# A hand-written order of issue for the first three units and the token weights, replaced by another

## The chip, the cores and the metric

The kernel runs on one core of one Trainium2 chip. The metric is device time in microseconds (us) for one launch; lower is better. Engines in the text: TensorE (PE; its weight loads are PEld), VectorE (DVE), ScalarE (ACT), GpSimd (POOL) and SyncE (SP), which issues almost all DMAs.

## What is computed

A linear attention with a decaying state (RWKV-6) feeds a mixer of two MLPs. Cut to what matters:

```python
batch, n_heads, seq, head_dim = (4, 8, 768, 48)
d_tok, d_ch = (256, 1536)
for t in range(S):
    kt, vt, rt, wt = (k[:, :, t], v[:, :, t], r[:, :, t], w[:, :, t])
    cur = np.einsum('bhd,bhe->bhde', u[None] * kt, vt)
    y[:, :, t] = np.einsum('bhd,bhde->bhe', rt, state + cur)
    state = wt[:, :, :, None] * state + np.einsum('bhd,bhe->bhde', kt, vt)
x = np.ascontiguousarray(attn_out.transpose(0, 2, 1, 3)).reshape(B, S, H * D)
xt = x.transpose(0, 2, 1)
h = np.maximum(xt @ w_tok1, 0.0) @ w_tok2
u = x + h.transpose(0, 2, 1)
h2 = np.maximum(u @ w_ch1, 0.0) @ w_ch2
return (u + h2).astype(np.float32)
```

Everything is float32, except that the four weights arrive as 64-bit floats and are put together on the chip from their bits.

## The kernel before

**Units.** The 768 tokens of a batch are cut into three units of 256; a unit holds 16 groups of 64 tokens for pairs of heads. `unit(i)` returns a unit's steps as small functions. On VectorE: `ends` (L372, a running product of the decays from the back, and a reciprocal), `keys` (L382), `begins` (L385, the running product from the front), `queries` (L388), `own_put` (L400), `mask` (L274), and `updates`, called s0, s1, s2 in the order, one for each of the four 64-token steps of the state (L445 to L453; the last unit has three). On ScalarE: `own_u` (L278, four multiplies), `copied` (L293, two copies of the turned keys), `scaled` (L438 to L443, called t0, t1, t2: four small multiplies each, between one update and the next), `seen` (L331), `taken` (L349, three copies of the result into x) and `ranges` (L366 to L369, two checks of the running product, whose sums are read at the very end). On TensorE: `own_gram` and `gram` (L262), `tokens` (L292, eight transposes), `carry` (L308, the outer products), `before` (L322, the products with the state) and `after` (L343, the products within the group). One update needs `carry` and the multiplies before it, and the next multiplies need the update, so a unit's state is a chain VectorE, ScalarE, VectorE, and so on.

**Banks.** During the first three units, PSUM has two double banks for gram and y (pool `ps_g`), two banks for the turned keys and the first product of the mixer (`ps_m`), and one for `carry` (`ps_a`). So `before` of unit 0 takes the bank that `mask` of unit 0 frees, `before` of unit 1 the one that `taken` of unit 0 frees, and `carry` of a unit waits for the last update of the unit before.

**Weights.** `convert` (L200) handles 512 KB times two of raw weights at a time. Its steps are load (two DMAs on SP), exponent x (DVE, L214), mantissa m (DVE, L220), power p (ACT, L217), sum add (DVE, L226), signs g (ACT, L223) and put (DVE, L229 and twice L232). `to_tok` has three of them, for the two token weights; `to_ch` has those for the channel weights, of which the first is in the hand-written order up to its signs. In the names x0, m0, p0, add0, g0, put0 the digit is the conversion; 3 is the first of `to_ch`. A load waits until the raw place that it fills has been read.

**Mixer of batch 0.** `hidden(i, c)` (L744) adds the product of 128 tokens (chunk c of six; a unit gives two) to one of two halves i, and is followed by a rectifier on ScalarE. In the list h the calls are h[2c + i]. `back(c)` (L751 to L756) needs both rectified halves, `turn` (L762, L763) transposes the result, `up` (L772) and `down` (L783) are the channel MLP.

**Order.** `strict` (L78) fixes the order of issue on TensorE, VectorE, ScalarE and SP to the order of the list it is given; each engine runs its own instructions in that order and waits where an operand is late. The call at L943 gives the order for units 0 to 2, the token weights and the first products of the mixer. After it, PSUM is divided anew into six banks, and `interleaved` (L854) merges three lists for batch 0: the mixer, the attention of batch 1 (units 3 to 5), and the channel weights, by a small model of engine times (costs in us, needs and banks written with each piece). In that merged part the next `ends` takes the place of a running product that the `ranges` of unit 1 read, which is why the planner was given `("of", 0)`.

Of the kernel before, what the change touches and what calls it, by code (L numbers as in the profile page):

```python
# [18 lines left out]
AF = mybir.ActivationFunctionType  # L19
# [4 lines left out]
C = S // 128  # L24
UC = 2
UB = C // UC
# [10 lines left out]
DTOK, DCH = 256, 1536  # L37
# [15 lines left out]
def rwkv6_then_mixer(  # L53
# [429 lines left out]
    rooms, forms, formed = {}, {}, {}  # L483
# [255 lines left out]
    def mixing(bt, x_of, out_rows):  # L739
        h1 = mpool.tile([128, DTOK // 128, DM], f32, name="h1", bufs=1)  # L740
        xT = mpool.tile([128, DM // 128, S], f32, name="xT", tag="xT", bufs=1)
        zs, sums = {}, {}

        def hidden(i, c):  # L744
            if c == 0:
                sums[i] = ps_m.tile([128, DM], f32, name="h1_ps", tag="m")
            pe.matmul(sums[i], now["wtok1"][:, c, ts(i, 128)], x_of()[:, c, :], start=(c == 0), stop=(c == C - 1))  # L747
            if c == C - 1:
                act.activation(h1[:, i, :], sums.pop(i), AF.Relu)

        def back(c):  # L751
            ps = ps_m.tile([128, DM], f32, name="h_ps", tag="m")
            for i in range(DTOK // 128):
                pe.matmul(ps, now["wtok2"][:, i, ts(c, 128)], h1[:, i, :], start=(i == 0), stop=(i == DTOK // 128 - 1))
            x = x_of()
            dve.tensor_add(x[:, c, :], x[:, c, :], ps)  # L756

        def turn(c):

            ps = bank("xT_ps")[:, :DM].rearrange("p (m t) -> p m t", t=128)  # L760
            for m in range(DM // 128):
                pe.transpose(ps[:, m, :], x_of()[:, c, ts(m, 128)], ident)  # L762
            act.copy(xT[:, :, ts(c, 128)], ps)  # L763

        def up(s, jt, blocks=range(DM // 128)):
            if jt == 0 and 0 in blocks:
                zs[s] = now["z"][int((bt, s) != (0, 0))].rearrange("p (j t) -> p j t", j=NJ)
            if 0 in blocks:
                sums["z", s] = ps_m.tile([128, SEG], f32, name="z_ps", tag="m")
            ps = sums["z", s]  # L770
            for m in blocks:
                pe.matmul(ps, now["wch1"][:, m, ts(jt, 128)], xT[:, m, ts(s, SEG)],  # L772
                          start=(m == 0), stop=(m == DM // 128 - 1))
            if DM // 128 - 1 in blocks:
                act.activation(zs[s][:, jt, :], ps, AF.Relu)

        def down(s, n, jts):

            if jts[0] == 0:
                sums[n] = ps_m.tile([128, DM], f32, name="h2_ps", tag="m")  # L780
            ps = sums[n]
            for jt in jts:
                pe.matmul(ps, zs[s][:, jt, ts(n, 128)], now["wch2"][:, jt, :], start=(jt == 0), stop=(jt == NJ - 1))  # L783
            if jts[-1] == NJ - 1:
                o = mpool.tile([128, 2, DM], f32, name="o", bufs=1) if n == 0 else sums["o"]
                sums["o"] = o
                dve.tensor_add(o[:, n], x_of()[:, 2 * s + n, :], ps)
                sp.dma_start(out_rows(2 * s + n), o[:, n])

        return dict(hidden=hidden, back=back, turn=turn, up=up, down=down)  # L790

    now["z"] = halves

# [3 lines left out]
    def attention_pieces(i):  # L797
# [6 lines left out]
        def piece(f, name, *ops):  # L804
            return (i, name), f, ops
# [5 lines left out]
            return pieces if i == UB else ()  # L811

        loads = piece(lambda: load_rk(i + 1), "loads")
        ends = piece(e["ends"], "ends", ("DVE", 2.6, last("small", "large", "by3") + ((("of", 0),) if i == UB else ())))
        keys = piece(e["keys"], "keys", ("DVE", 1.25, k("ends")))
        small, large = (piece(e["ranges"][n], name, ("ACT", 1.4, k("ends"))) for n, name in enumerate(("small", "large")))
        begins = piece(e["begins"], "begins", ("DVE", 2.35, k("ends")))
# [36 lines left out]
    def interleaved(mix, *others, room=0.6, hurry=0.04, lead=(0.01, 0.2)):  # L854
# [57 lines left out]
        while any(streams):  # L912
# [14 lines left out]

    turned = mixing_of(0)
    h = [lambda i=i, c=c: turned["hidden"](i, c) for c in range(C) for i in range(DTOK // 128)]
    to_tok = conversion((wtok1, w_tok1, 2, 256), (wtok2, w_tok2, 2, 256), rooms=lambda n: (n % 2, n % 2))  # L930
    to_ch = conversion((now["wch1"], w_ch1, 1, 512), (now["wch2"], w_ch2, 4, 128), rooms=lambda n: (n % 2, 0, rks[2][:, ts(n % 2, PIECE)].bitcast(bf16)) if n else (2, 1))
    to_tok[0][0]()
# [7 lines left out]
    in_turn.update({pe.engine: None, dve.engine: None, act.engine: None, sp.engine: None})  # L940
    s0, s1, s2 = (e["updates"] for e in (e0, e1, e2))
    t0, t1, t2 = (e["scaled"] for e in (e0, e1, e2))
    strict(*e0["own_u"], e0["ends"], e0["own_gram"], e0["begins"], e0["keys"], e0["tokens"], *e0["copied"], e0["queries"], lambda: load_w(2),  # L943
           e0["gram"], *e1["own_u"], e1["ends"], e0["carry"], *e0["ranges"], e0["own_put"], e0["mask"], e1["own_gram"], s0[0], t0[1],
           x0, p0, s0[1], t0[2], m0, g0, e1["begins"], s0[2], t0[3], add0, s0[3], t1[0], e0["before"], e0["seen"], put0, load2,
           e1["keys"], e0["after"], *e2["own_u"], e1["tokens"], *e1["copied"], e1["queries"], e1["own_put"], e1["carry"], *e0["taken"],
           lambda: load_v(2), e1["gram"], e2["ends"], g1, s1[0], t1[1], e2["keys"], e2["tokens"], s1[1], t1[2], e2["own_gram"], *e2["copied"],
           e2["begins"], s1[2], t1[3], e1["mask"], load3, s1[3], t2[0], *h[:2], e2["carry"], e1["before"], h[2], e2["queries"], s2[0], t2[1],
           e2["own_put"], e1["seen"], s2[1], t2[2], e2["gram"], x1, p1, e1["after"], m1, s2[2], t2[3], e2["mask"], h[3], add1,
           e1["taken"][0], put1, to_ch[1][0], lambda: (load_w(3), load_rk(3), load_v(UB)), e2["before"], e2["seen"], *e1["taken"][1:],  # L950
           x2, s2[3], e2["after"], *h[4:8], *e2["taken"], m2, p2, x3, add2, g2, m3, h[8], h[10], h[9], h[11], p3, put2, add3, g3,
           to_ch[2][0], e1["ranges"][0])

    six_banks.close()
    ps_g, ps_m = None, six_banks.enter_context(tc.tile_pool(name="ps_m", bufs=6, space=bass.MemoryType.PSUM))
# [56 lines left out]
    def weights_in_turn():  # L1012

        each = [single(steps, n) for n, steps in enumerate(to_ch)]
        for n in range(1, len(each) - 2):
            each[n].insert(-1, each[n + 2].pop(0))
        first = sum(each, [])
        stored = [(("kept", i), lambda i=i: sp.dma_start(kept[i], (wtok1, wtok2)[i].rearrange("p c k -> p (c k)")), ()) for i in range(2)]
        ranges = [(("of", n), f, (("ACT", 1.4, ()),)) for n, f in enumerate((e1["ranges"][1], *e2["ranges"]))]
        formed = [e for n in range(HALF) for e in splits(0, n)]  # L1020
        late = [e for n in range(HALF) for e in splits(1, n)]
        return first[:1] + each[1] + ranges + sum(each[2:], []) + stored + formed + late[:1] + late[5:6] + late[1:5] + late[6:-5 * AFTER], late[-5 * AFTER:]

    AFTER = 2
    flagged = []
# [28 lines left out]
    def by_halves(b):  # L1054
# [60 lines left out]
        for i in range(DTOK // 128):  # L1115
            for c in range(C):
                plain["hidden"](i, c)
        for c in range(C):
            plain["back"](c)
            plain["turn"](c)  # L1120
# [60 lines left out]
```

## Time and profile before

| | us |
|---|---|
| median of 3 runs | 509.79 |
| lowest and highest run | 509.04 and 511.49 |
| the profiled execution, time | 511.19 |
| the profiled execution, span from first to last instruction | 509.5 |
| TensorE busy | 479.2 |
| VectorE busy | 382.2 |
| ScalarE busy | 266.9 |

The page cuts the span into 40 slices of 12.7 us and gives each engine's busy share in tenths; PEclk is the clock granted to TensorE, in tenths. A row of a timeline has the start, the duration, the engine, the line of the kernel, the operation, what it writes and reads, the shape, the number of instructions, and in square brackets how long the engine was idle ahead of it and what released it. In the waits of TensorE over the whole span, the longest are the first load and then waits in the first 35 us:

```profile
PE gram L262 <- DMA rk<-in_rk_dram: 8.2, 1, 8.2
PE y_ps L322 <- ACT before L443: 2.1, 1, 2.1
PE gram L262 <- issue: 1.9, 1, 1.9
PE o_ps L655 <- DVE x L664: 1.7, 2, 0.9
PE k_ps L292 <- issue: 1.7, 1, 1.7
PE gram L262 <- DVE at L400: 1.7, 2, 1.5
```

The columns are the total, the number of waits and the longest.

### The profile page before, as it was taken

How to read it: one execution, taken by the hardware profiler on the slowest of the kernel's cores; microseconds unless marked ns; L12 is line 12 of the kernel's file. 1: busy time of each engine (PE TensorE's matmuls, PEld its weight loads, DVE VectorE, ACT ScalarE, POOL GpSimd, SP SyncE). 2: the span in 40 equal slices, each digit the busy share in tenths (PEclk: the TensorE clock that was granted, in tenths of full speed). 3: DMA queues.
4: the chain of work that ended last, by engine and by line, in shares of the span. 5: the costliest groups of instructions: out<-in, count | busy, mean ns of one | idle time of the engine just before them, and what ended most of it. 6: DMA issues, size and time to landing. Idle time of an engine off the chain costs nothing.

```text
span 509.5 us, 12748 instructions
## 1 busy us (share of the span) xinstructions
PE 479.2 (94%) x5218; PEld 404.4 (79%) x5218; DVE 382.2 (75%) x588; ACT 266.9 (52%) x631; POOL 53.2 (10%) x58
## 2 busy tenths in 40 slices
PE   3489999999999999999999999999999999999995
PEld 3477578866687667998989957999989958999995
DVE  7997998997764588787986948787985906566562
ACT  3876977755554544456545234556555324253350
POOL 0000000000000000311302000302212101130230
PEclk9769999999999999999999999999999999999999
DMA  8842937774560673583846571473725441345231
GB/s 305 321 177 64 302 115 257 243 220 136 158 196 26 192 216 116 177 233 99 262 122 210 187 249 60 140 227 97 258 70 156 143 153 48 98 135 171 78 111 50
DMA packets 48975, 83.76 MB, mean 164 GB/s; under 512 B 4816, under 2 KB 40272, under 8 KB 48912
## 3 DMA queue, kind: packets, MB, share of 16 engines
q1 hardware_dynamic: 48768, 82.90, 51.6%
q8 instruction: 42, 0.69, 0.6%
q14 instruction: 21, 0.17, 0.1%
q10 hardware_dynamic: 144, 0.00, 0.0%
HBM read 71.87 MB, written 11.01 MB: 163 GB/s over the span
## 4 chain that ended last, share of the span: by engine, by line
PE 82%; DVE 8%; DMA 3%; ACT 3%; issue 2%; SPq 0%; DVEq 0%; ACTq 0%
PE h_ps L783 9%; PE z_ps L772 9%; PE joint_ps L612 8%; PE ends_ps L641 7%; PE ends_ps L643 7%; PE o_ps L655 7%; PE o_ps L657 7%; PE o_ps L656 6%; PE h_ps L593 4%; PE h_ps L586 3%; PE gram L262 3%; PE kv_ps L308 3%; PE y_ps L343 2%; PE y_ps L322 2%; PE h_ps L747 2%
## 5 line engine op out<-in xcount | busy, mean ns | idle before, releaser
L634 POOL TENSOR_TENSOR z_high<-z_high 128x384 fp32r<-128x384 f32 x48 | 52.0, 1086 | 441.2 <-ACT z_high L619 237.6
L613 ACT ACTIVATE mid<-joint_ps 128x384 f32<-128x384 f32 x72 | 34.9, 485 | 64.5 <-PE joint_ps L612 63.3
L626 DVE TENSOR_TENSOR ends_ps<-ends_ps,mid 128x384 f32<-128x384 f32 x72 | 40.6, 563 | 32.4 <-PE ends_ps L643 19.8
L612 PE MATMUL joint_ps<-z_more,forms 128*128 128x384 f32 x216 | 51.6, 347 | 0.8 <-DVE z_more L564 0.8
L655 PE MATMUL o_ps<-forms,z_high 128*128 128x384 f32 x144 | 49.7, 345 | 1.7 <-DVE x L664 1.7
L641 PE MATMUL ends_ps<-x_forms,forms 128*128 128x384 f32 x216 | 49.5, 337 | 0.8 <-DVE z_high L630 0.8
L772 PE MATMUL z_ps<-xT,wch 128*128 128x256 f32 x216 | 49.4, 383 | 0.8 <-ACT xT L763 0.8
L643 PE MATMUL ends_ps<-x_forms,ring 128*128 128x384 f32 x216 | 49.3, 337 | 0.0
L657 PE MATMUL o_ps<-forms,z_high 128*128 128x384 f32 x144 | 48.8, 339 | 0.2
L783 PE MATMUL h_ps<-wch,z 128*128 128x384 f32 x144 | 48.5, 490 | 0.0
L656 PE MATMUL o_ps<-ring,z_high 128*128 128x384 f32 x144 | 48.5, 336 | 0.0
L443 ACT ACTIVATE before<-state,to_end 112x48 f32<-112x48 f32 x148 | 37.3, 326 | 19.1 <-DVE state L453 19.0
L772 PEld LDWEIGHTS z_ps<-xT,wch 128*128 128x128 f32 x216 | 40.1, 190 | 6.6 <-ACT xT L763 1.0
L783 PEld LDWEIGHTS h_ps<-wch,z 128*128 128x128 f32 x144 | 26.8, 190 | 17.1
L612 PEld LDWEIGHTS joint_ps<-z_more,forms 128*128 128x128 f32 x216 | 38.3, 188 | 2.4 <-DVE z_more L564 1.1
L664 DVE SCALAR_TENSOR_TENSOR x<-o_ps,x 128x384 f32<-128x384 f32 x36 | 19.8, 549 | 27.0 <-PE o_ps L656 26.8
L641 PEld LDWEIGHTS ends_ps<-x_forms,forms 128*128 128x128 f32 x216 | 38.6, 188 | 1.5 <-DVE z_high L630 1.5
L643 PEld LDWEIGHTS ends_ps<-x_forms,ring 128*128 128x128 f32 x216 | 38.5, 188 | 0.0
L655 PEld LDWEIGHTS o_ps<-forms,z_high 128*128 128x128 f32 x144 | 27.0, 188 | 2.9 <-DVE x L664 2.5
L657 PEld LDWEIGHTS o_ps<-forms,z_high 128*128 128x128 f32 x144 | 27.0, 188 | 1.5 <-DVE x L665 1.5
L622 ACT ACTIVATE z_high<-z_high 128x384 fp32r<-128x384 f32 x48 | 25.3, 526 | 4.1
L656 PEld LDWEIGHTS o_ps<-ring,z_high 128*128 128x128 f32 x144 | 27.1, 188 | 0.0
(153 smaller groups left out, 931.1 us busy)
## 6 DMA issues: line engine op xcount, KB each, us to landing
ring<-third SPq DMA_DIRECT2D x144, 192.0 KB, 3.6
raw<-in_w_ch_dram SPq DMA_DIRECT2D x16, 512.0 KB, 4.9
rk<-in_rk_dram SPq DMA_DIRECT2D x36, 192.0 KB, 5.5
near<-in_near_dram SPq DMA_DIRECT2D x8, 768.0 KB, 4.7
w<-in_w_dram SPq DMA_DIRECT2D x10, 520.5 KB, 3.7
vt<-in_v_dram SPq DMA_DIRECT2D x12, 384.0 KB, 3.5
out_dram<-x SPq DMA_DIRECT2D x18, 192.0 KB, 3.0
raw<-in_w_tok_dram SPq DMA_DIRECT2D x6, 512.0 KB, 9.5
```

The source lines that it names most:

```text
L443: act.mul(t[:ROWS, a], state[bt, g][:ROWS, a], by_last(c, j)[:, a:a + 1])
L612: pe.matmul(b, joint[m], xf[2][:, m], start=m == 0, stop=m == 2)
L613: act.mul(mid(jt), b, BASE / (BASE - 1.0))
L626: dve.tensor_add(a, a, mid(jt))
L634: pool.tensor_add(z_form(jt, 2), z_form(jt, 2).bitcast(f32), z_form(jt, 1).bitcast(f32))
L641: pe.matmul(a, up[m], xf[0][:, m], start=m == 0, stop=False)
L643: pe.matmul(a, low[:, m], xf[1][:, m], start=False, stop=m == 2)
L655: pe.matmul(a, z[0], up, start=first, stop=False, skip_group_check=True)
L656: pe.matmul(a, z[1], held[bt, s, half, 1, jt], start=False, stop=last, skip_group_check=True)
L657: pe.matmul(b, z[2], joint, start=first, stop=last, skip_group_check=True)
L772: pe.matmul(ps, now["wch1"][:, m, ts(jt, 128)], xT[:, m, ts(s, SEG)], start=(m == 0), stop=(m == DM // 128 - 1))
L783: pe.matmul(ps, zs[s][:, jt, ts(n, 128)], now["wch2"][:, jt, :], start=(jt == 0), stop=(jt == NJ - 1))
```

## The change

The list in the call of `strict` is replaced by another one with the same steps. Three things move across its end or change shape: the rectifier of the mixer's first product becomes a step of its own (`rectified`), so that it can stand apart from the last product; `ranges` of units 1 and 2, three of which were pieces for the planner (`("of", n)`), are all in the list now; and so the planner's `ends` of unit 3 no longer has `("of", 0)` among its needs. The loads of the next units (`load_w`, `load_v`, `load_rk`), which stand in SP's order, are placed one by one. By engine, the order of VectorE in the new list is: ends 0, begins 0, keys 0, ends 1, queries 0, own_put 0, x0, s0[0], keys 1, s0[1], begins 1, s0[2], own_put 1, mask 0, s0[3], m0, queries 1, s1[0], ends 2, s1[1], keys 2, s1[2], add0, mask 1, s1[3], put0, begins 2, s2[0], queries 2, s2[1], own_put 2, s2[2], m1, x1, mask 2, add1, x2, put1, m2, m3, add2, x3, put2, add3. That of TensorE: own_gram 0, tokens 0, carry 0, gram 0, own_gram 1, tokens 1, before 0, carry 1, gram 1, after 0, tokens 2, before 1, own_gram 2, after 1, carry 2, h[0], h[1], h[3], h[2], gram 2, before 2, h[4], after 2, h[5] to h[11]. SP issues w2, w3, v2, v3, the raw data of conversions 2 and 3, rk3, and the raw data of the next two channel conversions.

```diff
--- before.py
+++ after.py
@@ -745,8 +745,9 @@
             if c == 0:
                 sums[i] = ps_m.tile([128, DM], f32, name="h1_ps", tag="m")
             pe.matmul(sums[i], now["wtok1"][:, c, ts(i, 128)], x_of()[:, c, :], start=(c == 0), stop=(c == C - 1))
-            if c == C - 1:
-                act.activation(h1[:, i, :], sums.pop(i), AF.Relu)
+
+        def rectified(i):
+            act.activation(h1[:, i, :], sums.pop(i), AF.Relu)
 
         def back(c):
             ps = ps_m.tile([128, DM], f32, name="h_ps", tag="m")
@@ -787,7 +788,7 @@
                 dve.tensor_add(o[:, n], x_of()[:, 2 * s + n, :], ps)
                 sp.dma_start(out_rows(2 * s + n), o[:, n])
 
-        return dict(hidden=hidden, back=back, turn=turn, up=up, down=down)
+        return dict(hidden=hidden, rectified=rectified, back=back, turn=turn, up=up, down=down)
 
     now["z"] = halves
 
@@ -811,7 +812,7 @@
             return pieces if i == UB else ()
 
         loads = piece(lambda: load_rk(i + 1), "loads")
-        ends = piece(e["ends"], "ends", ("DVE", 2.6, last("small", "large", "by3") + ((("of", 0),) if i == UB else ())))
+        ends = piece(e["ends"], "ends", ("DVE", 2.6, last("small", "large", "by3")))
         keys = piece(e["keys"], "keys", ("DVE", 1.25, k("ends")))
         small, large = (piece(e["ranges"][n], name, ("ACT", 1.4, k("ends"))) for n, name in enumerate(("small", "large")))
         begins = piece(e["begins"], "begins", ("DVE", 2.35, k("ends")))
@@ -927,6 +928,7 @@
 
     turned = mixing_of(0)
     h = [lambda i=i, c=c: turned["hidden"](i, c) for c in range(C) for i in range(DTOK // 128)]
+    rectified = [lambda i=i: turned["rectified"](i) for i in range(DTOK // 128)]
     to_tok = conversion((wtok1, w_tok1, 2, 256), (wtok2, w_tok2, 2, 256), rooms=lambda n: (n % 2, n % 2))
     to_ch = conversion((now["wch1"], w_ch1, 1, 512), (now["wch2"], w_ch2, 4, 128), rooms=lambda n: (n % 2, 0, rks[2][:, ts(n % 2, PIECE)].bitcast(bf16)) if n else (2, 1))
     to_tok[0][0]()
@@ -940,16 +942,18 @@
     in_turn.update({pe.engine: None, dve.engine: None, act.engine: None, sp.engine: None})
     s0, s1, s2 = (e["updates"] for e in (e0, e1, e2))
     t0, t1, t2 = (e["scaled"] for e in (e0, e1, e2))
-    strict(*e0["own_u"], e0["ends"], e0["own_gram"], e0["begins"], e0["keys"], e0["tokens"], *e0["copied"], e0["queries"], lambda: load_w(2),
-           e0["gram"], *e1["own_u"], e1["ends"], e0["carry"], *e0["ranges"], e0["own_put"], e0["mask"], e1["own_gram"], s0[0], t0[1],
-           x0, p0, s0[1], t0[2], m0, g0, e1["begins"], s0[2], t0[3], add0, s0[3], t1[0], e0["before"], e0["seen"], put0, load2,
-           e1["keys"], e0["after"], *e2["own_u"], e1["tokens"], *e1["copied"], e1["queries"], e1["own_put"], e1["carry"], *e0["taken"],
-           lambda: load_v(2), e1["gram"], e2["ends"], g1, s1[0], t1[1], e2["keys"], e2["tokens"], s1[1], t1[2], e2["own_gram"], *e2["copied"],
-           e2["begins"], s1[2], t1[3], e1["mask"], load3, s1[3], t2[0], *h[:2], e2["carry"], e1["before"], h[2], e2["queries"], s2[0], t2[1],
-           e2["own_put"], e1["seen"], s2[1], t2[2], e2["gram"], x1, p1, e1["after"], m1, s2[2], t2[3], e2["mask"], h[3], add1,
-           e1["taken"][0], put1, to_ch[1][0], lambda: (load_w(3), load_rk(3), load_v(UB)), e2["before"], e2["seen"], *e1["taken"][1:],
-           x2, s2[3], e2["after"], *h[4:8], *e2["taken"], m2, p2, x3, add2, g2, m3, h[8], h[10], h[9], h[11], p3, put2, add3, g3,
-           to_ch[2][0], e1["ranges"][0])
+    strict(e0["ends"], e0["own_u"][0], e0["begins"], e0["own_u"][1], e0["own_u"][2], e0["own_u"][3], e0["own_gram"], e0["keys"], e0["ranges"][0],
+           e0["ranges"][1], e1["ends"], e0["tokens"], e0["queries"], e1["own_u"][0], e0["own_put"], e0["copied"][1], e0["copied"][0], e1["own_u"][1],
+           e0["carry"], e1["own_u"][2], e0["gram"], e1["own_u"][3], x0, s0[0], e1["keys"], t0[1], s0[1], e1["own_gram"], e1["begins"], t0[2],
+           e2["own_u"][0], e1["tokens"], s0[2], e1["own_put"], e1["copied"][0], t0[3], e0["mask"], s0[3], e1["copied"][1], m0, p0, e0["before"],
+           e0["seen"], e1["carry"], e2["own_u"][1], e1["queries"], t1[0], s1[0], e1["gram"], g0, e2["own_u"][2], e2["own_u"][3], lambda: load_w(2),
+           e0["after"], t1[1], e0["taken"][0], e2["ends"], s1[1], e2["keys"], t1[2], e2["tokens"], s1[2], e0["taken"][1], t1[3], e0["taken"][2],
+           lambda: load_w(3), add0, e1["mask"], e1["before"], s1[3], e2["copied"][0], put0, e2["own_gram"], e2["copied"][1], g1, e2["begins"],
+           lambda: load_v(2), e1["seen"], e1["after"], e2["carry"], t2[0], e1["ranges"][0], e1["taken"][0], h[0], e1["taken"][1], lambda: load_v(UB),
+           h[1], s2[0], e2["queries"], h[3], load2, t2[1], s2[1], t2[2], e2["own_put"], h[2], s2[2], e1["taken"][2], m1, x1, e2["gram"], t2[3],
+           e2["before"], p1, e2["seen"], h[4], e2["ranges"][0], load3, e2["mask"], e2["after"], e2["taken"][0], h[5], h[6], e2["taken"][1], add1,
+           h[7], e2["taken"][2], x2, p2, put1, h[8], m2, h[9], m3, g2, h[10], add2, lambda: load_rk(3), to_ch[1][0], x3, put2, rectified[0], h[11],
+           add3, rectified[1], to_ch[2][0], p3, g3, e2["ranges"][1], e1["ranges"][1], s2[3])
 
     six_banks.close()
     ps_g, ps_m = None, six_banks.enter_context(tc.tile_pool(name="ps_m", bufs=6, space=bass.MemoryType.PSUM))
@@ -1016,10 +1020,9 @@
             each[n].insert(-1, each[n + 2].pop(0))
         first = sum(each, [])
         stored = [(("kept", i), lambda i=i: sp.dma_start(kept[i], (wtok1, wtok2)[i].rearrange("p c k -> p (c k)")), ()) for i in range(2)]
-        ranges = [(("of", n), f, (("ACT", 1.4, ()),)) for n, f in enumerate((e1["ranges"][1], *e2["ranges"]))]
         formed = [e for n in range(HALF) for e in splits(0, n)]
         late = [e for n in range(HALF) for e in splits(1, n)]
-        return first[:1] + each[1] + ranges + sum(each[2:], []) + stored + formed + late[:1] + late[5:6] + late[1:5] + late[6:-5 * AFTER], late[-5 * AFTER:]
+        return first[:1] + each[1] + sum(each[2:], []) + stored + formed + late[:1] + late[5:6] + late[1:5] + late[6:-5 * AFTER], late[-5 * AFTER:]
 
     AFTER = 2
     flagged = []
@@ -1115,6 +1118,7 @@
         for i in range(DTOK // 128):
             for c in range(C):
                 plain["hidden"](i, c)
+            plain["rectified"](i)
         for c in range(C):
             plain["back"](c)
             plain["turn"](c)
```

## The prediction

> **What bounds the kernel now.** I read the page's slices first, then busy time by window, the chain of waits, the timelines of VectorE, TensorE and ScalarE up to 75 us, and last the DMA issues with their landing times.
>
> ```profile
> PE   3489999999999999999999999999999999999995
> DVE  7997998997764588787986948787985906566562
> ...
> PEclk9769999999999999999999999999999999999999
> ```
>
> TensorE is full from the sixth slice on. In the windows (us; then busy us and count of PE, PEld, DVE, ACT, POOL; granted clock; DMA share; GB/s):
>
> ```profile
> 18.00:20.00 2.00, 1.61 (x63) 1.54 (x63) 1.65 (x3) 2.00 (x7) 0.00 (x0) 0.86 1.05 385
> 20.00:22.00 2.00, 0.09 (x2) 0.00 (x0) 2.00 (x3) 1.44 (x4) 0.00 (x0) 0.50 1.04 389
> 28.00:30.00 2.00, 2.00 (x78) 1.77 (x80) 1.97 (x3) 1.71 (x5) 0.00 (x0) 0.58 1.02 392
> 32.00:34.00 2.00, 1.32 (x8) 1.21 (x8) 2.00 (x3) 1.58 (x8) 0.00 (x0) 0.77 0.03 12
> 38.00:40.00 2.00, 2.00 (x38) 1.04 (x38) 0.00 (x0) 0.00 (x0) 0.00 (x0) 0.52 0.00 0
> 70.00:120.00 50.00, 50.00 (x553) 39.21 (x552) 45.63 (x60) 34.21 (x71) 0.00 (x0) 1.00 0.62 197
> ```
>
> From 70 us TensorE has no hole, so the change can only move the moment at which the dense part begins. Before that VectorE is the engine without holes; its timeline has three that matter, here with the two rows that follow them:
>
> ```profile
> 18.35 0.35 DVE L453 TENSOR_TENSOR state<-before,kv_ps 112x192 f32<-112x192 f32 x1 [0.48 <-ACT before L443]
> 40.63 0.35 DVE L453 TENSOR_TENSOR state<-before,kv_ps 112x192 f32<-112x192 f32 x1 [2.70 <-PE kv_ps L308]
> ...
> 53.93 1.22 DVE L226 SCALAR_TENSOR_TENSOR z<-z,z 128x1024 f32<-128x1024 uint32 x1
> 56.02 0.69 DVE L229 TENSOR_TENSOR z<-z 128x1024 bf16<-128x1024 bf16 x1 [0.87 <-ACT z L223]
> 56.75 1.29 DVE L232 SCALAR_TENSOR_TENSOR wch<-z 128x512 f32<-128x512 f32 x2
> 57.96 1.01 DVE L756 TENSOR_TENSOR x<-x,h_ps 128x384 f32<-128x384 f32 x2
> ```
>
> TensorE's first transposes of the mixer (58.56) wait for that L756, and its last hole before the dense part is one row of its timeline:
>
> ```profile
> 65.92 1.13 PE L772 MATMUL z_ps<-xT,wch 128*128 128x256 f32 x4 [0.76 <-ACT xT L763]
> ```
>
> So the number sought is when VectorE reaches L756, with what ScalarE adds behind it.
>
> **VectorE's floor.** Nothing is added to or taken from VectorE. Steps from one start to the next in its timeline: ends 2.6 (L373, L377, L378), begins 2.24, keys 1.13, queries 1.15, own_put 1.2, mask 1.2, an update 0.26. A unit is 10.6 with four updates; three units, less one update that the last unit lacks, plus 0.2 for unit 0's scan in two halves, 31.7. The copies of L173 to L179: 0.6. A token conversion is 0.60 + 0.60 + 1.13 + 1.94 = 4.27, three are 12.8; the fourth conversion without its put 2.33. Sum 47.4. From the first scan at 3.81 it could end at 51.2; it ended at 55.15 (53.93 + 1.22). Of the 3.9 lost, 3.2 are the first two holes, the rest hand-overs of about 0.1, of which I leave 0.5 in the new order. The question is which waits the new order has.
>
> **The change, walked through by engine with the durations of before.**
> Up to 16.25 VectorE doesn't wait: ends, begins, keys of unit 0, then ends of unit 1 at about 10.6 (its w was issued at 2.68 and took 6.7, so landed at 9.4), queries, own_put, and the exponent of conversion 0 at 15.65 (raw issued by 5.8, 9.2 to 9.8 to landing: 15.4 to 15.6; a margin of 0.1 and a bound of 0.5 if it is late, taken at 0). The two ranges of unit 0 move to ScalarE's idle time between own_u (ends 8.4) and the rk of unit 1 (3.63 + 8.0 = 11.6): free, since before ScalarE idled 2.96 there; without that cover 2.54. The copies of kT end at 13.3 instead of 12.8, hidden because the first update comes at 16.25.
> From there to 23.2: keys 1, begins 1 and own_put 1 lie between the updates of unit 0, each long enough to cover the 0.95 of ScalarE's four multiplies: the 0.48 goes.
> TensorE has nothing between tokens of unit 1 (ends 18.8) and the across-product of unit 0, which waits for the mask (done 22.96) that frees its bank. Before, at 20.2 to 22.2, the clock was already 0.50, and here the hole is 4.2 us. At half clock the 48 products take 1.5 (28 took 1.12 at 22.21 but spread; the 64-row groups 1.96) and carry of unit 1 1.78 (row at 28.23): it ends at 26.3. VectorE, past mantissa and queries, wants it at 24.85: **wait one, 1.45** (0.6 at full clock, as ScalarE's multiplies then end it at 25.4).
> Ends of unit 2 follow (w2 landed at 13.04 + 11.4 = 24.5, the same issue or little later), one update, keys at 29.5. Its gram and within-product on TensorE at half clock end at 30.2; ScalarE's first copy of x stands ahead of the multiplies that the third update needs at 30.6: **wait two, 0.9** cold, 0 warm.
> Sum, mask 1, last update and put of conversion 0 run to 36.5, begins 2 to 38.7. TensorE: the across-product of unit 1 can't start before ScalarE's last copy of unit 0 frees the bank, 33.6. Four groups follow (across, own gram, within, carry 2): 4 x 1.08 at full clock, 37.9; 4 x 1.9 cold, 41.0. VectorE's update wants carry 2 at 38.7: **wait three, 0 to 2.35**; with the clock back halfway 0.5. This is the place of before's 2.70: there h[0] and h[1] (2.93 at half clock) stood ahead of carry 2, and now they stand behind it.
> After that I find no wait but 0.1 at mask 2. The last hidden products end about when put 1 allows (eight entries, 2.7), the backs (4.14 for three) fit before L756, so TensorE idles there a little over 1.
> **Moved DMAs on SP.** w3 (before 48.38) now goes at about 25, when queries 1 is done; v2, v3 wait for the two within-products (30 and 37 to 39); raw of conversion 2 and of 3 stand behind v3 and go at 38 to 40 instead of 22.99 and 26.80. They landed in 3.7 to 5.3, so by 45; their readers are at 46 and 49. rk3, four issues that were at 48.86, go before the next raw. From 50 to 66 before, the DMA share was 0.98 to 1.07, so an earlier w3 and rk3 takes load off. I price all this at 0; if v3 were 3 later, the exponent of conversion 2 would wait up to 2.
> **Ranges.** Before, ScalarE runs four ranges (1.27 step each) from 55.9, among the xT copies. Now two run right behind the signs of conversion 3, two earlier. The 0.87 at L229 goes, since its ScalarE part comes behind the earlier products; and of the 0.76 plus two 0.2 holes of TensorE I take 0.8. Lower bound 0: at 69.74 TensorE comes to the transposes of unit 3, which wait for VectorE's keys, and a lead over VectorE is lost there.
>
> **Sum.** 51.2 + 0.5 + 1.45 + 0.9 + 0.5 + 0.1 = 54.65, against 55.15: 0.5. With 0.87 it is 1.4 at L756, with 0.8 it is **2.2**. The profiled execution has a span of 509.5 and a time of 511.19; the runs' median, 509.79, is 1.4 below it. I take the difference from the median: **507.6**; from the profiled execution it would be 509.0.
>
> The granted clock falls at about 19.5 and 33.1 and returns at 29.6 and 39.9: steps of three, one and two times 3.4. [...]
>
> **Rivals.**
> *Warm.* The first busy stretch (23.0 on) restores the clock by 26.4 and the hole of about 2 before 33.6 doesn't cool it: waits two and three vanish, gain 2.2 + 1.4 = 3.6, **506.2**. [...] Against: the row at 33.1. [...]
> *Cold through carry 2.* Wait three in full: 2.2 - 1.85 = 0.35 gained, **509.4**. For it: before, the same stretch was cold from 33.1 to 39.9.
> *Slower: cold through the hidden products too.* Four of them now stand ahead of gram 2 on TensorE. If the clock is still 0.50 when they start (41.0), they take 1.43 each (2.86 for two in the chain of waits), so 5.7, gram 2 ends at 48.8, and mask 2, wanted at 45.4, waits 3.4: -3.0, **512.8**. It decides if half clock lasts beyond 41. Against: by then TensorE has run 7 us without a hole.
> *Given back.* VectorE is 91% busy from 70 to 120; if the list, planned anew without the three ranges, lets TensorE wait for a converted weight, the lead goes: **509.8**. Against: TensorE had no hole there.
>
> **How the numbers follow.** Forecast 0.40 (own range 506.7 to 508.7), warm 0.22, cold 0.20, slower 0.10, given back 0.08. The 0.5% that a measurement of this kernel can tell is 2.5 us, a bound at 507.2. Faster: warm 0.20 and the better half of the forecast 0.20, 0.40. Same: 0.22 of forecast and warm, cold 0.20, given back 0.07, 0.49. Slower: 0.11. The range for 8 in 10 runs from 505.0, warm with a full 0.8 and wait one at 0.6, to 511.0, into the slower case.
>
> **What would show it.** Right: VectorE's update at L453 waits near 25 about 1.5 for L308 and near 39 less than 2; L756 first starts at 56.5; no hole at L229; TensorE's first z_ps group without a ScalarE wait. Wrong: any other VectorE hole over 0.5 (raw late, above all), L756 at 58 or later, or TensorE holes between 66 and 120.

## The result: two groups of times, and the profile after

| | us |
|---|---|
| before, median of 20 runs | 509.29 (508.29 to 511.49) |
| changed, median of 20 runs | 517.71 (510.27 to 521.93) |
| ratio | 1.0115, 95% interval 1.0082 to 1.0148 |

The change makes the kernel slower. Its times fall in two groups with nothing between: four of the twenty runs at 510.27 to 511.06, sixteen at 516.45 to 521.93. The kernel before has one group. The ratio leaves some of the long runs out as disturbed and so understates what a median shows, 8.4 us.

The profile after caught a *short* execution (510.27, span 508.6). VectorE's timeline there, in the columns explained above, has these rows at the waits that the prediction walked through and at the first x add:

```profile
25.73 0.35 DVE L453 TENSOR_TENSOR state<-before,kv_ps 112x192 f32<-112x192 f32 x1 [0.75 <-ACT before L443]
...
30.59 0.35 DVE L453 TENSOR_TENSOR state<-before,kv_ps 112x192 f32<-112x192 f32 x1 [0.48 <-ACT before L443]
...
39.01 0.35 DVE L453 TENSOR_TENSOR state<-before,kv_ps 112x192 f32<-112x192 f32 x1 [1.30 <-PE kv_ps L308]
...
54.54 0.71 DVE L229 TENSOR_TENSOR z<-z 128x1024 bf16<-128x1024 bf16 x1
...
56.50 1.01 DVE L757 TENSOR_TENSOR x<-x,h_ps 128x384 f32<-128x384 f32 x2
```

The three waits of the walk are there, though none has the size that was predicted; the wait at L229 is gone, and the first x add (L756 before, L757 now) starts at 56.50, where the prediction put it. Behind it TensorE's timeline has other holes than before, where it waited 0.43 at the first of these places, nothing at the second and 0.76 for ScalarE at the third:

```profile
57.11 0.55 PE L763 MATMUL xT_ps<-ident,x 128*128 128x128 f32 x3 [1.60 <-DVE x L757]
...
64.12 0.55 PE L763 MATMUL xT_ps<-ident,x 128*128 128x128 f32 x3 [0.74 <-DVE x L757]
...
67.04 1.13 PE L773 MATMUL z_ps<-xT,wch 128*128 128x256 f32 x4 [1.18 <-DVE wch L232]
```

In the page's slices of 12.7 us they are the two eights of the fifth and sixth, which were nines before:

```profile
PE   3769889999999999999999999999999999999995
...
PEclk9879999999999999999999999999999999999998
```

So a short execution has its waits where the prediction's walk has them, and a loss behind L757 (experiment 2); the long ones must hold something that this profile doesn't show.

### The profile page after: what moved, and what is told of

It is laid out like the page before. It is cut to its first block, busy times and chain, and to the rows that moved or that the text cites. A ratio compares the mean times of both kernels' runs of the same rounds, so it can differ in the third digit from the quotient of the medians.

```text
span 508.6 us, 12746 instructions
## 1 busy us (share of the span) xinstructions
PE 477.8 (94%) x5218; PEld 404.5 (80%) x5218; DVE 382.1 (75%) x588; ACT 267.5 (53%) x631; POOL 53.3 (10%) x58
## 4 chain that ended last, share of the span: by engine, by line
PE 76%; DVE 7%; DMA 1%; ACT 1%; issue 1%; SPq 0%; DVEq 0%; ACTq 0%
PE z_ps L773 9%; PE joint_ps L612 8%; PE ends_ps L641 7%; PE ends_ps L643 7%; PE h_ps L784 7%; PE o_ps L655 7%; PE o_ps L657 7%; PE o_ps L656 6%; PE h_ps L586 5%; PE h_ps L593 4%; PE gram L262 2%; PE kv_ps L308 2%; PE y_ps L322 2%; PE y_ps L343 2%; DVE to_end L377 1%; DMA third<-ring 1%
## 5 line engine op out<-in xcount | busy, mean ns | idle before, releaser
L773 PE MATMUL z_ps<-xT,wch 128*128 128x256 f32 x216 | 49.6, 383 | 1.2 <-DVE wch L232 1.2
L773 PEld LDWEIGHTS z_ps<-xT,wch 128*128 128x128 f32 x216 | 40.1, 190 | 7.0 <-DVE wch L232 1.4
L443 ACT ACTIVATE before<-state,to_end 112x48 f32<-112x48 f32 x148 | 37.2, 325 | 12.3 <-DVE state L453 12.3
L612 PEld LDWEIGHTS joint_ps<-z_more,forms 128*128 128x128 f32 x216 | 38.3, 188 | 2.4 <-DVE z_more L564 1.1
L630 DVE SCALAR_TENSOR_TENSOR z_high<-ends_ps,z_high 128x384 fp32r<-128x384 f32 x48 | 26.3, 548 | 1.1 <-ACT z_high L619 1.0
```

The source lines that it names most:

```text
L443: act.mul(t[:ROWS, a], state[bt, g][:ROWS, a], by_last(c, j)[:, a:a + 1])
L612: pe.matmul(b, joint[m], xf[2][:, m], start=m == 0, stop=m == 2)
```

## The experiments

The texts quoted were each written before their run. "Theory I", from experiment 3 on: TensorE's program itself arrives by DMA in blocks, and one of them comes late when loads have just been issued.

**1. The changed kernel once more** (`a_again`), unaltered, to catch a long execution.

> The changed kernel unaltered, to see an execution of the long kind: its 20 times fall into two groups, 510.3 to 511.1 (4 of them) and 516 to 522 (16), and the profiled execution is of the first group. Theory T (TensorE's clock): the 7 us are lost before 70 us, half clock lasting beyond the hidden products, and the first back products come near 57 instead of 51.4. Rival D (a transfer): one stall of 5 to 8 us with the clock at 1.00, TensorE waiting for one late DMA or for an engine that waits for one, somewhere after 50 us. Rival I: the time is spread over the whole span.

517.87 (516.96 to 518.90, 4 runs), all long, and so is the profile. Its TensorE timeline between 42 and 54 us:

```profile
42.45 1.16 PE L262 MATMUL gram<-first 48*64 48x64 f32 x64 [0.40 <-DVE at L400]
43.41 0.55 PE L322 MATMUL y_ps<-before,first 48*64 48x48 f32 x24
48.63 1.32 PE L322 MATMUL y_ps<-before,first 48*64 48x48 f32 x40 [4.68 <-issue]
49.88 1.65 PE L747 MATMUL h_ps<-x,wtok 128*128 128x384 f32 x2
51.45 1.96 PE L343 MATMUL y_ps<-vt,at 64*64 64x48 f32 x64
53.34 5.35 PE L747 MATMUL h_ps<-x,wtok 128*128 128x384 f32 x14
```

In the middle of 64 equal products (L322 of unit 2), after the 24th, TensorE stands still for 4.68 us and waits for nothing that a semaphore shows ("issue"). In the short execution the same 64 products are one row:

```profile
43.02 1.13 PE L322 MATMUL y_ps<-before,first 48*64 48x48 f32 x64
```

Of the three theories of the text, the single stall (D) comes nearest, but it lies before 50 us, no late transfer shows as what ended it, and the clock falls behind it. The windows (columns as in the prediction) show the sequel: the clock is halved from about 47.7, and the two hidden products at 49.88 take 1.65 where the short execution's take 0.91.

```profile
44.00:47.00 3.00, 0.00 (x0) 0.00 (x0) 3.00 (x4) 0.99 (x1) 0.00 (x0) 1.00 1.06 387
47.00:48.00 1.00, 0.00 (x0) 0.00 (x0) 0.96 (x3) 0.00 (x0) 0.00 (x0) 0.85 1.02 205
48.00:52.00 4.00, 3.37 (x62) 2.20 (x65) 3.02 (x6) 1.31 (x3) 0.00 (x0) 0.50 1.02 250
```

VectorE then waits 4.61 at L229 for ScalarE's signs, which stand behind unit 2's results, and the first x add comes at 63.25, 6.75 later than in the short execution:

```profile
57.29 0.69 DVE L229 TENSOR_TENSOR raw<-raw 128x1024 bf16<-128x1024 bf16 x1 [4.61 <-ACT raw L223]
...
63.25 1.01 DVE L757 TENSOR_TENSOR x<-x,h_ps 128x384 f32<-128x384 f32 x2
```

During the hole the DMA share is 1. What fills it stands in SP's own timeline of this run:

```profile
30.00 8.66 SPq L149 DMA_DIRECT2D vt<-in_v_dram  x2
38.77 0.92 SPq L211 DMA_DIRECT2D raw<-in_w_tok_dram  x2
39.74 0.95 SPq L211 DMA_DIRECT2D z<-in_w_ch_dram  x2
40.73 2.69 SPq L141 DMA_DIRECT2D rk<-in_rk_dram  x4
```

The second v load waits for the products that free its buffer (unit 1's L343) and holds up the three loads behind it; all four go out between 38.3 and 43.4.

The page after counts a DMA queue of a kind of its own, "q8 instruction: 42, 0.69": 42 packets and 0.69 MB, so 16.4 KB each. Counting TensorE's products in the traces, the holes that end in issue lie, where a kernel that adds none has them, behind the same numbers: 221, 348, 476, 602, 730 and 856 or 857, which is 126 to 128 apart, with their weight loads 252 to 256 records. The 24th product of that L322 is number 856 or 857 (some traces lack a record). Two more holes that end in issue, behind 64 and 512, are not in this series: they stand ahead of a unit's transposes (L292), and what ends them isn't shown. In the DMA view of this run from 37 to 45.8 us (columns: packets, MB, share):

```profile
q1 hardware_dynamic: 1005, 2.16, 71.4%
```

and from 45.8 to 47.5:

```profile
q1 hardware_dynamic: 164, 0.56, 106.0%
q8 instruction: 1, 0.02, 3.5%
```

The next block comes only behind 2.16 MB of data. Its packet starts at 46.21 and takes 0.95, and TensorE goes on 1.5 after its end. In the short execution it starts at 38.63, 0.3 us after v's issue has ended there (29.17 + 9.19), and TensorE doesn't wait.

**2. The list alone and the planner alone.** `b_list_only` has the new list, but unit 2's ranges and the second of unit 1 go to the planner as before; `c_planner_only` has the old list and the new planner's input.

```diff
 b_list_only, against the changed kernel
-           e2["before"], p1, e2["seen"], h[4], e2["ranges"][0], load3, ...
+           e2["before"], p1, e2["seen"], h[4], load3, ...
-           ..., p3, g3, e2["ranges"][1], e1["ranges"][1], s2[3])
+           ..., p3, g3, s2[3])
+        ranges = [(("of", n), f, (("ACT", 1.4, ()),)) for n, f in enumerate((e1["ranges"][1], *e2["ranges"]))]
 c_planner_only, against the kernel before
-           to_ch[2][0], e1["ranges"][0])
+           to_ch[2][0], *e1["ranges"], *e2["ranges"])
-        ranges = [(("of", n), f, (("ACT", 1.4, ()),)) for n, f in enumerate((e1["ranges"][1], *e2["ranges"]))]
```

> The new list, but the second range of unit 1 and both of unit 2 back as pieces for the planner, and ends of unit 3 again behind them, so that the planner's merged list is that of before. If the hand-written list makes the long executions (T, or a DMA of the list), about four in five are 516 to 519 here too. If the planner's new merge makes them (D in the dense part), all are 507 to 510, because L757 still starts at 56.5 and the 1.18 wait for L232 goes.

> The old list with all ranges at its end, and the planner as changed (no ranges as pieces, ends of unit 3 without that need). If the list makes the long executions, all are 509 to 511. If the merge makes them, most are 515 to 520.

`b_list_only`: 516.09 (511.24, and three at 515.79 to 516.55), the hole in the same place:

```profile
48.80 1.32 PE L322 MATMUL y_ps<-before,first 48*64 48x48 f32 x40 [4.95 <-issue]
```

`c_planner_only`: 510.47 (509.99 to 511.66, 10 runs), ratio 1.0028, interval 1.0017 to 1.0039, one group. So the list makes the long executions, and the planner by itself costs 1.4. Without the ranges among its pieces it puts `ends` of unit 3 (L377) at 61.04, in front of the last x adds and of the put of conversion 1 of the mixer's weights (L232), both of which TensorE waits for; before it stood behind them:

```profile
61.04 2.33 DVE L377 TENSOR_TENSOR_SCAN to_end<-w,starts 112x1041 f32<-112x1041 f32 x1
...
63.57 0.95 DVE L757 TENSOR_TENSOR x<-x,h_ps 128x384 f32<-128x384 f32 x2
...
65.58 0.68 DVE L229 TENSOR_TENSOR raw<-raw,first 128x1024 bf16<-128x1024 bf16 x1
66.30 1.29 DVE L232 SCALAR_TENSOR_TENSOR wch<-raw 128x512 f32<-128x512 f32 x2
```

(VectorE's timeline of the changed kernel, short execution.) In `c_planner_only` TensorE's holes behind it are 1.70 for an x add (64.53) and 0.20 for a converted weight (67.36).

**3. Where the block boundary lies.** If the hole is a boundary between blocks, added instructions move it to an earlier product. `d_pad10` and `e_pad56` give TensorE 10 and 56 more small products of the identity (two load-and-product pairs each by the trace); `f_list_pad10` does the first with the list alone.

```diff
+    pad = bank("pad")
+    for _ in range(10):
+        pe.matmul(pad[:64, :64], ident[:48, :64], ident[:48, :64], start=True, stop=True)
```

> The changed kernel with 10 products of the identity (20 weight loads and 20 matmuls in the trace) ahead of everything on TensorE, in the time in which it waits for the first load. [...] Rival P (the place): the hole belongs to these L322 products or to what they read; it stays after 24 of them and most executions are 516 to 519.

> The same with 56 products, 112 pairs, so that the block begins 16 pairs later than in the changed kernel and its request comes later by 0.5. Theory I: every execution has the hole, 40 instead of 24 products into L322 of unit 2, and is 516 to 520; none at 510. Rival P: four in five long, the hole after 24 products.

> The list alone (ranges with the planner as before) with the 10 products ahead. Theory I: no long execution; without the planner's new merge, which cost about 1.2 by itself in the run of the planner alone, 508 to 509.5, that is at or a little under the kernel before. Rival P: 516.

`d_pad10` 513.58 (512.83 to 514.02), `e_pad56` 526.84 (523.76 to 530.05), `f_list_pad10` 513.11 (511.27 to 515.56, 8 runs). TensorE's holes that end in issue, one timeline row of each in that order (four lines are added to the kernel, so L326 is L322 and L751 is L747):

```profile
48.86 4.14 PE L751 MATMUL h_ps<-x,wtok 128*128 128x384 f32 x12 [2.03 <-issue]
```

```profile
61.20 0.89 PE L326 MATMUL y_ps<-before,first 48*64 48x48 f32 x24 [4.79 <-issue]
```

```profile
49.66 5.62 PE L751 MATMUL h_ps<-x,wtok 128*128 128x384 f32 x12 [2.58 <-issue]
```

With 112 more pairs the hole moves from behind 24 to behind 40 of the 64 products: 16 later, which is 128 less 112. Counted with the added products, the holes of all three stay in the series: 221, 348 or 349, 476, 604, 730 and 984 (the one at 512 does not: in `d_pad10` it is at 532). So this is the boundary of a block and nothing in the products. (`e_pad56` missed the 516 to 520 expected because its products ran in 11.83 us inside unit 0's own gram and not in idle time.) With 20 pairs the block for number 857 comes early enough (38.20 and 39.05), and the next one, whose packet starts at 46.45 and 46.74 (DMA share 0.97 and 1.02 from 40 to 50 us), is late by 2.0 to 2.6 in the hidden products. That was not foreseen: where theory I had `d_pad10` at 509.5 to 511.5 and `f_list_pad10` at 508 to 509.5, they came out at 513.6 and 513.1.

**4. The kernel before again** (`g_before_again`), for a second profile beside the changed kernel's.

> The kernel before, unaltered, for the profile of a usual execution: the profiled one shown was at 511.19, near the upper end. Expected a span of 507.5 with L756 first at 56.5 to 57.5, less half clock or shorter waits for blocks before 40.

509.08 (508.72 to 511.06). Its VectorE timeline at the places shown of before:

```profile
38.25 0.35 DVE L453 TENSOR_TENSOR state<-before,kv_ps 112x192 f32<-112x192 f32 x1 [0.17 <-PE kv_ps L308]
...
50.38 0.69 DVE L229 TENSOR_TENSOR raw<-raw 128x1024 bf16<-128x1024 bf16 x1 [0.92 <-ACT raw L223]
...
54.48 0.69 DVE L229 TENSOR_TENSOR z<-z 128x1024 bf16<-128x1024 bf16 x1 [0.93 <-ACT z L223]
...
56.41 1.01 DVE L756 TENSOR_TENSOR x<-x,h_ps 128x384 f32<-128x384 f32 x2
```

The 2.70 us that the prediction saw at L308 belong to that one execution: there the clock was halved a second time, from 33.1 to 39.9 us; here it is full from 30.6 on, the wait is 0.17, and the first x add comes at 56.41, not 57.96. That is 1.55 and not 2.53 earlier, because VectorE now waits 0.92 for ScalarE's signs of conversion 2 (50.38), where the first profile has no wait. A usual execution of before reaches it where the short ones of the changed kernel do.

**5. Three ways to move the block or the loads a little.** `h_swap` puts carry 2 ahead of unit 1's last products; `i_swap_list` does so with the list alone; `j_raw3_early` moves z's load.

```diff
 h_swap, i_swap_list
-           lambda: load_v(2), e1["seen"], e1["after"], e2["carry"], t2[0], ...
+           lambda: load_v(2), e2["carry"], e1["seen"], e1["after"], t2[0], ...
 j_raw3_early
-           lambda: load_w(3), add0, ...
+           lambda: load_w(3), load3, add0, ...
-           ..., e2["ranges"][0], load3, e2["mask"], ...
+           ..., e2["ranges"][0], e2["mask"], ...
```

> The changed kernel with carry 2 (L308, and what VectorE does with it) ahead of unit 1's L322 and L343 in the list, so that the products which free v's buffer stand some 28 pairs later on TensorE. [...] No execution of 515 us or more, all between 508.5 and 511; no hole at L322 of unit 2 that ends in issue; the wait for carry 2 of 1.3 us is gone, the 1.2 us that TensorE waits for the converted weight stays. Rival (the long executions come from something else in the order, such as the clock): four executions in five stay at 516 to 522, as they were.

> The new list alone (ranges of unit 2 and the second of unit 1 as planner pieces, as in the kernel before), with the same exchange of carry 2. Theory I: neither the late block nor the planner's merge is left, so 507.5 to 509, equal to the kernel before or up to 1.5 below it, no execution over 513. Rival (the order is slow by itself): 511 or more.

> The changed kernel with z's third load (1.05 MB) issued at about 25 us, behind the third block of weights, and no longer at 39.7. Theory I: the data ahead of the block in the queues falls from 2.5 MB to 1.4 MB, so the hole at L322 of unit 2 shrinks from 4.7 to at most 2 us, and the long executions from 516 to 522 to 511 to 514; a block needed near 28 us is up to 2 us later. Rival (the hole doesn't depend on the data in front of it): hole and times stay.

`h_swap` 513.89 (510.79 to 518.57, 10 runs): the hole is still there in the profile (4.30), in fewer executions (four of ten over 516). The v load moved to 40 us, but so, it seems, did the block (the packet of `i_swap_list`, which has the same order, starts at 40.36, that of the short execution at 38.63): a race shifted, not ended. `i_swap_list` 511.95 (509.75 to 513.26, 9 runs): its block came at 40.36, in front of the loads' data, and no execution was long; but the update then waits for ScalarE (1.49), and the expected 507.5 to 509 was not reached. `j_raw3_early` 518.88 (516.48 to 520.28): the hole stays at 4.59. My bytes were wrong there. With z gone, rk's four loads (0.79 MB) move up into its place, and the block, at 48.48, stood behind them too.

**6. All four loads out of the way.** `k_loads`: z behind the third w, the third raw load behind add 0, rk and v of unit 3 behind the next raw load. `l_loads_list`: the same with the list alone. `m_loads_v` and `n_loads_list_v`: as these, with unit 2's v put ahead of the raw load.

```diff
-           lambda: load_w(3), add0, e1["mask"], ...
+           lambda: load_w(3), load3, add0, load2, e1["mask"], ...              (k, l)
+           lambda: load_w(3), load3, lambda: load_v(2), add0, load2, ...       (m, n)
-           ..., e1["taken"][1], lambda: load_v(UB),
+           ..., e1["taken"][1],
-           ..., add2, lambda: load_rk(3), to_ch[1][0], x3, ...
+           ..., add2, to_ch[1][0], lambda: load_rk(3), lambda: load_v(UB), x3, ...
```

> The changed kernel with its work unaltered and four loads elsewhere on SP: z's third load behind the third block of weights (about 27 us), the third raw load behind add 0 (about 33), and unit 3's rk and v behind the next raw load (after 45). Nothing is then issued between about 36 and 45 us, where TensorE asks for the block that begins at count 857. Theory I: no hole ended by issue at L322 of unit 2, no long execution; times 509 to 511.5 (the planner's merge is still in, 1.2 to 1.7). If rk or v come too late for unit 3, a wait on DMA shows there instead. Rival (the order of the engines' work makes the hole, whatever the loads do): a hole of over 4 us at L322 and four executions in five over 515.

> The new list alone (the ranges of unit 2 and the second of unit 1 left to the planner, as before) with the same four loads moved. Theory I: no late block and no merge, 507.5 to 509.5, at or a little below the kernel before. Rival (the order is slow by itself): 511 or more.

> As k_loads, with unit 2's v loaded ahead of the third raw load (about 30 us and no longer 33.6), since the products of carry 2 (L308) waited there for v. Theory I: no wait on DMA at L308, VectorE waits for carry 2 for 1.0 to 1.8 us instead of 4.06; no hole over 1.5 us ended by issue between 38 and 60; its x adds begin at 56 to 57.5; all executions between 509 and 511.5, like the short ones of the changed kernel, since only the planner's merge is left. Rival (a hole of another kind remains in this order): over 513 or two groups of times.

> The new list alone, without the merge, with the loads of m_loads_v. Theory I: 507.8 to 509.5, level with the kernel before to within half a per cent, which would say that the list's order of computation is by itself worth nothing and that the loss is all in the late block and the merge. Rival (the new order's computation is itself slower): 510.5 or more.

`k_loads` 514.96 (514.85 to 515.42, 5 runs), `l_loads_list` 513.20 (512.56 to 513.84, 6 runs), `m_loads_v` 514.55 (514.28 to 514.79, 4 runs), `n_loads_list_v` 511.69 (510.62 to 512.44, 5 runs). The hole of over 4 us and the two groups are gone in all four: with `m_loads_v` the runs lie within 0.5 us of each other. But the times are 2.7 to 6.4 above the medians of before beside them, and the ranges expected were missed. In k and l, unit 2's v came late behind the raw load (TensorE waits 0.45 and 2.71 for it at L308). In m and n that wait is gone, and what is left shows in `m_loads_v`'s TensorE timeline:

```profile
40.05 1.52 PE L308 MATMUL kv_ps<-vt,kT 64*64 64x48 f32 x30 [1.07 <-issue]
...
48.47 0.80 PE L322 MATMUL y_ps<-before,first 48*64 48x48 f32 x40 [0.46 <-issue]
```

and on VectorE:

```profile
41.68 0.35 DVE L453 TENSOR_TENSOR state<-before,kv_ps 112x192 f32<-112x192 f32 x1 [3.35 <-PE kv_ps L308]
...
47.73 1.31 DVE L274 COPY_PREDICATED at<-before_it,gram 128x1024 f32<-128x1024 uint8 x1 [1.63 <-PE gram L262]
...
60.53 1.01 DVE L757 TENSOR_TENSOR x<-x,h_ps 128x384 f32<-128x384 f32 x2
```

The raw load, now at 32.77, delays the block before (behind product 730; its packet starts at 37.69 behind that load's data and in the short execution at 35.22). With the clock granted at 0.50 from 35.8 to 46.0, VectorE's waits are 3.35 and 1.63; how much of them is the clock's and how much the block's isn't shown. The new order makes add 0 (L226), which frees the raw buffer, 9.7 us later than before (31.49 in this run, 21.84 in `g_before_again`). Before, it could go at 23.12, and the packets that came behind its data and z's (27.47 and 31.75 in `g_before_again`) were still in time; no place for it that delays no block was found in the new order.

**7. One piece of the order in the kernel before** (`o_before_p3`): ScalarE's exponent plane of conversion 3 ahead of the rectified halves, which is what removes the wait at L229.

```diff
-           x2, s2[3], ..., add2, g2, m3, h[8], h[10], h[9], h[11], p3, put2, add3, g3,
+           x2, s2[3], ..., add2, g2, m3, p3, h[8], h[10], h[9], h[11], put2, add3, g3,
```

> The kernel before with one step moved: ScalarE makes the exponent plane of conversion 3 (p3, L217) ahead of the two rectified halves of the hidden products and no longer behind them. It is the part of the new order that takes away VectorE's wait of 0.93 us at L229 (54.48), without any load, product or planner step moved. Theory: p3 at about 50.4, the halves at 51.4 and 51.9, g3 at 52.4; the wait at L229 goes, the first x add (L756) comes 0.7 to 1.0 us earlier than 56.41, back (L754) starts 0.6 later and has over 3 us to spare: 508.2, 0.5 to 0.9 below the kernel before. Rival (TensorE, which runs without a hole from 57.0 to 64.4, sets the time there and not VectorE): no change, or up to 0.6 slower.

508.37 (507.05 to 510.48, 12 runs) against 509.05 (17 runs of before beside it); ratio 0.9994, interval 0.9982 to 1.0006. The wait is gone, and the x add is 1.4 earlier than 56.41 (some 0.4 of it from the stretch before, where this execution was ahead):

```profile
53.04 0.69 DVE L229 TENSOR_TENSOR z<-z 128x1024 bf16<-128x1024 bf16 x1
...
54.98 1.01 DVE L756 TENSOR_TENSOR x<-x,h_ps 128x384 f32<-128x384 f32 x2
```

In this execution 0.8 of the lead is lost again at 299 us, where TensorE waits 0.78 for a load of z_high. The medians differ by 0.68 in the expected direction; by the interval a gain isn't shown. No version clearly beat the kernel before.

**What the profiles add up to.** Taking `g_before_again` as zero, the start of the first x add and that of a scan in the dense part (L377, at 178.34 us there):

```
                    first x add   L377 near 178   merged planner
changed, short          +0.1          +1.5           yes
a_again                 +6.8          +8.5           yes
b_list_only             +6.9          +6.9           no
c_planner_only          +0.4          +1.9           yes
d_pad10                 +1.8          +3.4           yes
f_list_pad10            +3.4          +3.4           no
m_loads_v               +4.1          +5.6           yes
n_loads_list_v          +3.2          +3.2           no
i_swap_list             +1.6          +3.1           no
o_before_p3             -1.4          -1.3           no
```

Every kernel with the new planner input loses 1.4 to 1.7 between the two columns, and those without it lose nothing, with one exception. In the profile of `i_swap_list` the clock was granted at 0.50 from 59.30 to 62.71, TensorE's four products at 59.03 (L755) take 2.50 where others take 1.46, and VectorE waits 1.38 for them at L757 (63.83); so it loses 1.5 for a reason of its own. The rest of the difference is there by the first x add.

## Why the prediction was wrong

- **"What bounds the kernel now"** was right: all that the change does is done by the first x add and the merge behind it, and a microsecond there is a microsecond in the dense part (the table).
- **VectorE's floor and the three waits.** The places were right, and L757 came at 56.50. The sizes were not: 0.75, 0.48 and 1.30 measured for 1.45, 0.9 and 0.5. That the sums agree, 2.5 for 2.85, is luck, because the errors cancel. In the short execution the clock was full from 24.24 to 31.07, where the prediction had it at half until about 30, so the first wait ended with ScalarE's multiplies (L443) and not with carry 1 (L308); it was at half from 31.07 to 37.89, ahead of the third wait.
- **The gain of 1.4 at L756** was taken from one profile and subtracted from the median of all runs. The profiled execution, in which the clock fell a second time, was itself 1.5 late there (57.96; 56.41 in the second profile). Against a usual execution the new order gains nothing: +0.1. What failed here is "I take the difference from the median", which set the forecast 1.4 too low; most of the miss has another source.
- **The ranges, 0.8,** had the wrong sign: "given back", the rival held at 0.08, is what happened, through a hole of 1.18 at L773 for a converted weight and late x adds. It costs 1.4 to 1.5, shown by the planner alone.
- **The moved DMAs on SP, "I price all this at 0",** is the step of the prediction that made the miss: about 6.8 in four runs of five. The times of issue were right (38 to 40), and their readers' waits small (0.23 for z in the short execution). What was not looked at is who else uses the queues then: TensorE's own program. Before, SP issued nothing between about 29 and 44 us, and this cover went.

So: a usual 509.1, plus 0.1, plus 1.5 is 510.7 (the short group: 510.27 to 511.06), and plus 6.8 is 517.5 (all runs' median: 517.71). Of the rivals about the clock neither "warm" nor "cold through carry 2" came about whole: in the short execution it was full from 24.24 on, as "warm" has it, and then at half again until 37.89. "Cold through the hidden products" came true in its form in the long executions, the clock being at 0.50 when some of them ran, but from the late block and not from carry 2. That a busy stretch of 3.4 us brings the clock back, as "warm" reckons (23.0 to 26.4), no run shows: in the profile of before it fell at 33.09, behind a hole of 1.73 that ended at 32.68, and came back at 39.91, 7.2 after that hole; in the short execution it came back 5.3 after one (32.54 and 37.89).

That the late block is the cause of the long group rests on three things: the hole's place moves with the count of instructions (3), its packet is seen behind the data (1), and the group vanishes where the loads are elsewhere (6). Not settled: what the order would be worth with every block in time and the old planner input, since each way of moving the loads made another block late or lost on another wait; and what sets the start of the next block's packet. In `before`, with no data in the queues for over 5 us, it started some 16 products ahead of the block before it (37.97) and 43 into it (46.97); in `e_pad56` (33.29) it started 83 into it.

## What to carry to other kernels

A move of loads can cost time on an engine that reads none of them, as here, where a block of instructions came only behind the loads' data: look where TensorE enters a new block (here the holes are 126 to 128 products apart), when that block's packet starts (here, with the data queues empty, from some 16 products ahead of the block before to 43 into it) and what loads are issued ahead of it. In `m_loads_v`, with none issued between 34.5 and 50.2 us, the hole of over 4 us was gone. One profile is one execution: before taking a wait in it as a gain, see whether it is there in a second one, above all where the granted clock differs. And where a planner fits pieces around hand-ordered work, taking pieces from it moves all the others, so its part of a change is run by itself.

## What was not expected of the hardware

- A block of 16.4 KB for TensorE came behind 2.2 MB of data, 7.6 us later than in the short execution (46.21 and 38.63). The packet itself took 0.95 and 1.22, so the delay lies ahead of it. In `before` and in the short execution, up to 60 us, the six packets that started with no data under way took 0.93 to 1.29. Where TensorE stood waiting for one, the first product started 1.4 after its end (18.24 and 19.63, 26.94 and 28.34 in the short execution) and 1.5 in `a_again` (47.16 and 48.63).
- A hole of 4.7 goes with a loss of 6.8. Some 0.4 of it is there before the hole (the update at 39.39 and not 39.01), and behind it TensorE's clock is at 0.50 from 47.7 to 54.5 us in `a_again`. In the traces of before and of the short execution the clock's stretches at 0.50 last 10.24 and 6.83, and 3.41 and 6.83 us. In `m_loads_v`, where it was at 0.50 from 35.8, it came back at 46.0, 6.0 after the last hole ended (40.05); what brings it back is not shown.
